# Softmax factors of an attention block sent through device memory instead of through matmuls, in a fused attention and two-layer MoE kernel

## The chip, the core and the metric

One core of one Trainium2 chip runs the kernel. The metric is the device time of one execution in microseconds. The kernel before took 609.13 us (median of three runs, 607.92 to 609.83).

## What is computed

Causal attention over 2 batches, 12 heads, 448 positions and 64 values a head; then two feed-forward blocks over the 896 tokens. All is float32 at the ends.

```python
def _attn_ref(q, k, v):
    scores = scale * np.matmul(q, k.transpose(0, 1, 3, 2))
    scores = np.where(mask, -1000000000.0, scores)
    scores = scores - np.max(scores, axis=-1, keepdims=True)
    attn = np.exp(scores)
    attn = attn / (np.sum(attn, axis=-1, keepdims=True) + 1e-09)
    return np.matmul(attn, v).astype(np.float32)
```

The first block is x @ w_in (768 to 2048), a clipped square, @ w_out; the second normalizes by the root of the mean square, multiplies silu(x @ w_gate) by x @ w_val (768 to 1536) and goes through w_out2.

The change is about one factor of this, 1 / (sum of the exponentials + 1e-9): one number for each head and query position.

## The kernel before

The attention goes by **groups** g of two heads (j = 0, 1), twelve in all. The 448 positions are cut into four chunks c of 112. A group is done in three **units** u = 0, 1, 2 (chunk 3; chunks 2 and 0; chunk 1), and a loop over n = 3g + u issues, in one iteration, steps of several units: the scores of unit n + 1 (TensorE, L267), the maxima of unit n (VectorE, L274) and its exponentials with their sums (ScalarE, L282), the copies out of PSUM of unit n − 2 (L316 on ScalarE, L318 on VectorE), and the transposes of unit n − 1 (TensorE, L298). With u = 2 the product with v of the group before is issued (`pv`, L346), which needs all its transposed exponentials. The order on each engine is the order of the code; nothing is reordered. Scores turn through four PSUM banks, two for each unit, so the scores of a unit need the exponentials of the unit two before to be done; the transposes and the spread turn through three other banks (`tring`).

The factor takes this way. With u = 0 VectorE adds 1e-9 to the sums and takes the reciprocal (`factor`, L324 and L325): a tile `rs` of 112 partitions (positions within a chunk) by 2 heads by 4 chunks. But the product with v stands with 64 partitions for each head and the positions along the row, so the factor is needed as a row, the same on 64 partitions. With u = 1 `spread` (L332) does this by eight matmuls: a column of `rs`, repeated 64 times, against the identity matrix. Each appears as two matmul instructions in the trace, 16 for a group. ScalarE copies the result to `rb` (L334). With the next u = 0 `xsplit` multiplies the product with v by `rb` on VectorE (L352), in place, and GpSimd splits it into a high and a low part (L353, L354), inputs of the first block.

SP issues all DMAs, in the order of the code, and holds at each one until what it waits for is there: q and k of a group two ahead (L239, L240, with u = 1, when the scores have read the buffer), v (L234, after `pv`), and weight blocks of 768 KB (L137), each when a stage buffer is free. While the attention runs, a few weight blocks are already loaded and split (L157 to L190), a share of a block in each group. From the last unit on, matmuls of the first block (L361) are issued between the attention's steps, and then the blocks follow: L361, L551, L666.

Of the kernel before, what the change touches and what calls it, by code (L numbers as in the profile page):

```python
# [10 lines left out]
F32 = mybir.dt.float32  # L11
# [4 lines left out]
ALU = mybir.AluOpType  # L16
# [24 lines left out]
def kernel(  # L41
# [14 lines left out]
    nc = tc.nc  # L56
    B, H, D, S = qT.shape
    P = 128
    C = 112
    NCH = S // C  # L60
# [14 lines left out]
    small = ctx.enter_context(tc.tile_pool(name="small", bufs=4))  # L75
    psum = ctx.enter_context(tc.tile_pool(name="psum", bufs=1, space=bass.MemoryType.PSUM))

    pst = psum.tile([P, 8, 512], F32, name="ps")

    def bank(n):  # L80
        return pst[:, n]

    ident = const.tile([P, P], F32, name="ident")
# [10 lines left out]
    TMO = STO + NST * 2 * NK * P  # L94
    AF = Arena(const, TMO + 2 * S, F32, "af")
# [6 lines left out]
    X = [AR.at(XO + h * 2 * NK * S, 2, NK, S) for h in range(2)]  # L102
    G = [AF.at(GO + h * NM * S, NM, S) for h in range(2)]
    stage = [AF.at(STO + i * 2 * NK * P, 2 * NK * P) for i in range(NST)]
    tmp = [AF.at(TMO + i * S, S) for i in range(2)]
# [11 lines left out]
    PTO = PO + 2 * NPC  # L117
    PTs = [AF.at(PTO + i * 2 * NTB * C, 2, NTB, C) for i in range(2)]
    XFO = PTO + 4 * NTB * C
    rb = AF.at(XFO, S)  # L120
    mask = AF.at(XFO + S, S)
    assert XFO + 2 * S <= STO
    poff = [0, C, 3 * C, 6 * C]
# [1 line left out]
    def b32(ap):  # L125
        return ap.bitcast(F32)
# [102 lines left out]
    NG = B * NP  # L229
    NN = NG * NU  # L230

    def load_v(g):
        if g < NG:
            nc.sync.dma_start(out=vraw[g % 2][:C], in_=v[g // NP, g % NP])  # L234
# [7 lines left out]
    def scale_q(g, eng):  # L242
        if g < NG:
            q = qraw[g % NQ]
            eng.tensor_scalar(out=q, in0=q, scalar1=float(D) ** -0.5, scalar2=1.0, op0=ALU.mult, op1=ALU.mult)  # L245

    sring = deque([0, 1, 2, 3])
    tring = deque([4, 5, 6])

    def turn(ring):  # L250
        ring.rotate(-1)
        return bank(ring[-1])
# [68 lines left out]
    def factor(g):  # L321
        sums = stat.pop(g)[1]
        rs = small.tile([P, 2, NCH], F32, tag="rs", name="rs")
        nc.vector.tensor_scalar(out=rs[:C], in0=sums[:C], scalar1=1e-9, scalar2=None, op0=ALU.add)  # L324
        nc.vector.reciprocal(rs[:C], rs[:C])  # L325
        return rs

    def spread(rs):
        t = turn(tring)
        for c in range(NCH):  # L330
            for j in range(2):
                nc.tensor.matmul(t[D * j:D * (j + 1), c * C:(c + 1) * C], lhsT=rs[:C, j, c:c + 1].to_broadcast([C, D]),  # L332
                                 rhs=ident[:C, :C], start=True, stop=True, skip_group_check=True)
        nc.scalar.copy(rb, t[:, :S])  # L334

    xbank = {}

    def pv(g):
        i = g % 2
        PT = PTs[i]  # L340
        xbank[g] = xb = bank(7)
        parts = [(0, 1, C, 3 * C), (0, 11, 0, C)] + [(kc, 4 * kc, kc * C, (NCH - kc) * C) for kc in range(1, NCH)]
        for n, (kc, blk, o, w) in enumerate(parts):
            for j in range(2):
                src = PT[:C, j].rearrange("p a d -> p (a d)")[:, blk * C:blk * C + w]
                nc.tensor.matmul(xb[D * j:D * (j + 1), o:o + w], lhsT=vraw[i][:C, j, kc, :], rhs=src,  # L346
                                 start=(n == 0), stop=(n == len(parts) - 1), skip_group_check=True)

    def xsplit(g):
        b, p = divmod(g, NP)  # L350
        xb = xbank.pop(g)
        nc.vector.tensor_tensor(out=rb, in0=xb[:, :S], in1=rb, op=ALU.mult)  # L352
        nc.gpsimd.tensor_scalar(out=X[b][:, 0, p], in0=rb, scalar1=1.0, scalar2=1.0, op0=ALU.mult, op1=ALU.mult)  # L353
        nc.gpsimd.tensor_tensor(out=X[b][:, 1, p], in0=rb, in1=b32(X[b][:, 0, p]), op=ALU.subtract)  # L354


    def mm3(out, w, x, ks=None):
# [88 lines left out]
    for n in range(last):  # L446
        g, u = divmod(n, NU)
        if n + 1 < NN:
            scores(n + 1)
        side = nc.vector if u == 2 else nc.scalar  # L450
        old = 2 <= n < NN + 2
        if u == 1:
            scale_q(g + 2, nc.gpsimd)
            load_qk(g + 3)
        if n < NN:
            maxima(n, 0)
            maxima(n, 1)
        if old and u == 1:
            evac(n - 2, 0, nc.scalar)
        if n < NN:  # L460
            exps(n, 0)
        if n < NN and u == 0:
            exps(n, 1)
        if old and u != 1:
            evac(n - 2, 0, nc.scalar)
            evac(n - 2, 1, side)
        if n < NN and u:
            exps(n, 1)
        if 0 < g < NG and u == 2:
            pv(g - 1)  # L470
            load_v(g + 1)
        if 1 <= n <= NN:
            transposes(n - 1)
        if u == 0:
            if g > 1:
                xsplit(g - 2)
            if g:
                frs = factor(g - 1)
        elif u == 1 and g:
            spread(frs)  # L480
            if g == NG:
                pv(g - 1)
        elif g == NG:
            xsplit(g - 1)
        if u == 2:
            w_pace(RATE[0])
        if n >= NN - 1:
            push_in(n - NN + 1, 0)
            pump(NK)
        flush()  # L490


    if True:
# [65 lines left out]
        rs = AF.at(4 * S, S)  # L559
# [98 lines left out]
        for dm in range(NK):  # L658
            w_need(2 * NM + 2 * NF + 2 * dm + 2)
            for h in range(2):  # L660
                w_pace(1)
                ob = nbank()
                for kk in range(NF):
                    x = (A0, A1)[h][kk]
                    for i, (a, c) in enumerate(((0, 0), (0, 1), (1, 0))):
                        nc.tensor.matmul(ob[:, :S], lhsT=w2[dm][:, kk // NK, a, kk % NK], rhs=x[:, c],  # L666
                                         start=(kk == 0 and i == 0), stop=(kk == NF - 1 and i == 2))
# [47 lines left out]
```

## Time and profile before

| | |
|---|---|
| median of the runs | 609.13 us (607.92 to 609.83) |
| span of the profiled execution | 607.3 us |
| matmuls busy | 597.2 us, 98% |
| VectorE busy | 385.7 us, 64% |
| ScalarE busy | 287.0 us, 47% |
| GpSimd busy | 162.9 us, 27% |
| share of the DMA engines | 32.5% on the queue of SP |

The span is the time from the first to the last instruction of one execution; the time of a run also holds what lies around it. [...] PE is the matmuls, PEld the weight loads, DVE VectorE, ACT ScalarE, POOL GpSimd, SP the engine that issues the DMAs. The attention takes about the first 110 us of the span, the rest is the two blocks. [...]

### The profile page before, as it was taken

The page shows a single profiled execution, that of the slowest core. Times are in us where ns is not written, and L with a number is a line of the kernel's source. Part 1 is how long each engine was busy: PE and PEld are TensorE (multiplying, and loading weights), DVE is VectorE, ACT ScalarE, POOL GpSimd, SP SyncE. Part 2 cuts the span into 40 slices and gives each one's busy share as a digit, 9 for nine tenths or more (in the row PEclk, how much of TensorE's full clock was granted, in tenths as well). Part 3 has the DMA queues.
Part 4 walks back from the last instruction along what each step waited for, and adds up shares of the span by engine and source line. Part 5 has one row for each costly group of instructions (what it writes and reads, how often), then busy time and mean ns, then how long its engine had stood idle before and what let it go on. Part 6 is the DMA issues. An engine that isn't in the chain of part 4 may idle for free.

```text
span 607.3 us, 8643 instructions
## 1 busy us (share of the span) xinstructions
PE 597.2 (98%) x3316; PEld 524.9 (86%) x3316; DVE 385.7 (64%) x643; ACT 287.0 (47%) x567; POOL 162.9 (27%) x118
## 2 busy tenths in 40 slices
PE   6999999999999999999999999999999999999997
PEld 4666668899999989998899999999999999999996
DVE  4777784368787646655694688887767666964000
ACT  4888886266766744445433433343333333543100
POOL 3234242324344313230122103222222222132200
PEclk9999999999999999999999999999999999999999
DMA  8245322034454523431132103334333333182100
GB/s 305 83 140 145 93 84 68 0 105 158 163 201 155 165 81 120 158 104 53 52 105 97 59 1 104 105 112 140 113 104 105 104 105 105 52 254 91 38 30 32
DMA packets 16698, 65.06 MB, mean 107 GB/s; under 512 B 2000, under 2 KB 6608, under 8 KB 16656
## 3 DMA queue, kind: packets, MB, share of 16 engines
q1 hardware_dynamic: 16656, 64.50, 32.5%
q8 instruction: 26, 0.43, 0.3%
q14 instruction: 16, 0.13, 0.1%
HBM read 61.74 MB, written 2.75 MB: 106 GB/s over the span
## 4 chain that ended last, share of the span: by engine, by line
PE 97%; DVE 1%; ACT 1%; DMA 0%; issue 0%; SPq 0%; DVEq 0%; ACTq 0%
PE ps L361 48%; PE ps L551 18%; PE ps L666 14%; PE ps L267 5%; PE ps L298 5%; PE ps L346 4%; PE ps L332 2%; DMA af<-in_qT 0%; PE ps L577 0%; DVE ar L568 0%; ACT af L369 0%; DVE ps L163 0%; DVE af L176 0%; DVE ps L157 0%; ACT ar L504 0%
## 5 line engine op out<-in xcount | busy, mean ns | idle before, releaser
L361 PE MATMUL ps<-ar 128*128 128x448 f32 x1440 | 293.3, 366 | 0.0
L361 PEld LDWEIGHTS ps<-ar 128*128 128x128 f32 x1440 | 270.3, 188 | 21.8 <-issue 0.4
L190 POOL TENSOR_TENSOR ar<-af,ar 128x768 fp32r<-128x768 f32 x68 | 128.7, 1892 | 346.6 <-ACT ar L182 346.6
L551 PE MATMUL ps<-ar 128*128 128x448 f32 x576 | 118.1, 366 | 0.4 <-DVE ar L568 0.3
L551 PEld LDWEIGHTS ps<-ar 128*128 128x128 f32 x576 | 108.0, 188 | 10.2 <-DVE ar L568 0.9
L182 ACT CAST ar<-af 128x768 fp32r<-128x768 f32 x68 | 60.2, 886 | 98.5 <-DVE af L176 95.6
L666 PE MATMUL ps<-ar 128*128 128x448 f32 x432 | 87.7, 365 | 0.0
L666 PEld LDWEIGHTS ps<-ar 128*128 128x128 f32 x432 | 81.2, 188 | 6.4
L172 ACT ACTIVATE af<-af 128x768 f32<-128x768 f32 x62 | 56.7, 914 | 25.5 <-DMA af<-in_w_out 15.2
L163 DVE SCALAR_TENSOR_TENSOR ps<-af,ps 128x768 int32<-128x768 int32 x62 | 59.6, 961 | 12.2 <-ACT af L172 9.6
L157 DVE TENSOR_SCALAR ps<-af 128x768 int32<-128x768 int32 x62 | 59.1, 953 | 8.2 <-DMA af<-in_w_out 6.5
L176 DVE SCALAR_TENSOR_TENSOR af<-af,ps 128x768 int32<-128x768 int32 x62 | 59.1, 954 | 5.3
L282 ACT ACTIVATE af<-ps,nm 112x336 f32<-112x336 f32 (+2 forms) x96 | 46.9, 502 | 8.5 <-DVE nm L274 8.5
L274 DVE CUSTOM_DVE_ANT_0 ps<-ps,af 112x336 f32<-112x336 f32 (+2 forms) x96 | 41.5, 473 | 12.2 <-PE ps L267 11.1
L505 DVE TENSOR_TENSOR ar<-af,ar 128x448 fp32r<-128x448 f32 x32 | 23.3, 732 | 40.3 <-ACT ar L504 40.3
L374 DVE SCALAR_TENSOR_TENSOR af<-af,ps 128x448 f32<-128x448 f32 x32 | 19.8, 618 | 38.8 <-ACT af L370 38.8
L504 ACT CAST ar<-af 128x448 fp32r<-128x448 f32 x32 | 18.0, 566 | 49.8 <-PE ps L551 49.8
L267 PE MATMUL ps<-af 64*112 64x448 f32 (+3 forms) x192 | 36.2, 462 | 4.6 <-DVE af L245 4.4
L369 ACT ACTIVATE af<-ps,half 128x448 f32<-128x448 f32 x32 | 20.1, 628 | 26.1 <-PE ps L361 26.1
L669 ACT COPY af<-ps 128x448 f32<-128x448 f32 x12 | 6.4, 533 | 53.5 <-PE ps L666 27.4
L298 PE MATMUL ps<-ident,af 112*112 112x112 f32 x240 | 31.6, 272 | 0.0
L298 PEld LDWEIGHTS ps<-ident,af 112*112 112x112 f32 x240 | 23.8, 137 | 8.0 <-issue 4.2
(52 smaller groups left out, 381.4 us busy)
## 6 DMA issues: line engine op xcount, KB each, us to landing
af<-in_w_out SPq DMA_DIRECT2D x28, 768.0 KB, 4.3
af<-in_w_in SPq DMA_DIRECT2D x16, 768.0 KB, 4.3
af<-in_w_gate SPq DMA_DIRECT2D x12, 768.0 KB, 4.2
af<-in_w_val SPq DMA_DIRECT2D x12, 768.0 KB, 4.2
af<-in_kT SPq DMA_DIRECT2D x12, 224.0 KB, 2.7
af<-in_qT SPq DMA_DIRECT2D x12, 224.0 KB, 3.1
af<-in_v SPq DMA_DIRECT2D x12, 224.0 KB, 2.6
out_T<-af SPq DMA_DIRECT2D x12, 224.0 KB, 2.0
```

Source lines behind the costliest of these rows:

```text
L157: nc.vector.tensor_scalar(out=out, in0=t, scalar1=29, scalar2=0, op0=ALU.logical_shift_right, op1=ALU.bitwise_or)
L163: nc.vector.scalar_tensor_tensor(out=t, in0=words(n, 1, I32), scalar=-2 ** 31, in1=t, op0=ALU.bitwise_and, op1=ALU.bitwise_or)
L172: nc.scalar.mul(c, c, 2.0 ** -112)
L176: nc.vector.scalar_tensor_tensor(out=words(n, 0, I32), in0=words(n, 1, I32), scalar=3, in1=part.pop(n), op0=ALU.logical_shift_left, op1=AL ...
L182: nc.scalar.copy(dst[:, 0, :], value(n))
L190: nc.gpsimd.tensor_tensor(out=dst[:, 1, :], in0=value(n), in1=b32(dst[:, 0, :]), op=ALU.subtract)
L267: nc.tensor.matmul(bs[j][:C, o:o + (c + 1) * C], lhsT=q[r, c * C:(c + 1) * C], rhs=k[r, :(c + 1) * C], start=True, stop=True, skip_group_c ...
L282: nc.scalar.activation(Pn[:C, j, poff[c]:poff[c] + w], sbank[n][j][:C, o:o + w], ACTF.Exp, bias=nm[:C, j, c:c + 1], scale=-1.0, accum_out= ...
L298: nc.tensor.transpose(bs[j][:C, o:o + C], Pn[:C, j, poff[c] + kc * C:poff[c] + (kc + 1) * C], ident[:C, :C])
L361: nc.tensor.matmul(out, lhsT=w[:, a, k * P:(k + 1) * P], rhs=x[:, c, k], start=(k == 0 and n == 0), stop=(k == NK - 1 and n == 2))
L551: nc.tensor.matmul(ybs[dm][:, :S], lhsT=w[:, a, dm * P:(dm + 1) * P], rhs=t[:, c], start=(n == 0 and i == 0), stop=(n == NM - 1 and i == 2))
L666: nc.tensor.matmul(ob[:, :S], lhsT=w2[dm][:, kk // NK, a, kk % NK], rhs=x[:, c], start=(kk == 0 and i == 0), stop=(kk == NF - 1 and i == 2))
```

## The change

`spread` with its matmuls and its copy is gone. `factor` itself sends `rs` to a buffer in device memory, `row`, two heads by 448 numbers, of which there are two in turn. The position of a number in a row is p·4 + c (p within a chunk, c the chunk), so each partition writes four numbers in one piece: 112 partitions by two heads give 224 pieces of 16 bytes. Two loads, one for each head, read a row back with a partition step of zero: 64 partitions get the same 448 numbers. The target is one of two buffers, `rbs`; one is the old `rb`, the other lies in a temporary row of the first block, `tmp[1]`. The loads wait for the store. `xsplit` reads the factor in steps of four numbers (the order of the rows) and writes its product to `tmp[0]`, not in place.

```diff
+    dram = ctx.enter_context(tc.tile_pool(name="dram", bufs=2, space=bass.MemoryType.DRAM))
...
-    rb = AF.at(XFO, S)
+    rbs = [AF.at(TMO + S, S), AF.at(XFO, S)]
...
         nc.vector.reciprocal(rs[:C], rs[:C])
-        return rs
-
-    def spread(rs):
-        t = turn(tring)
-        for c in range(NCH):
-            for j in range(2):
-                nc.tensor.matmul(t[D * j:D * (j + 1), c * C:(c + 1) * C], lhsT=rs[:C, j, c:c + 1].to_broadcast([C, D]),
-                                 rhs=ident[:C, :C], start=True, stop=True, skip_group_check=True)
-        nc.scalar.copy(rb, t[:, :S])
+        row = dram.tile([2, S], F32, tag="row", name="row")
+        nc.sync.dma_start(out=row.rearrange("j (p c) -> p j c", c=NCH), in_=rs[:C])
+        for j in range(2):
+            nc.sync.dma_start(out=rbs[g % 2][D * j:D * (j + 1)], in_=row[j].partition_broadcast(D))
...
-        nc.vector.tensor_tensor(out=rb, in0=xb[:, :S], in1=rb, op=ALU.mult)
-        nc.gpsimd.tensor_scalar(out=X[b][:, 0, p], in0=rb, scalar1=1.0, scalar2=1.0, op0=ALU.mult, op1=ALU.mult)
-        nc.gpsimd.tensor_tensor(out=X[b][:, 1, p], in0=rb, in1=b32(X[b][:, 0, p]), op=ALU.subtract)
+        rb = rbs[g % 2]
+        xn = tmp[0]
+        nc.vector.tensor_tensor(out=xn.rearrange("p (c i) -> p c i", c=NCH),
+                                in0=xb[:, :S].rearrange("p (c i) -> p c i", c=NCH),
+                                in1=rb.rearrange("p (i c) -> p c i", c=NCH), op=ALU.mult)
+        nc.gpsimd.tensor_scalar(out=X[b][:, 0, p], in0=xn, scalar1=1.0, scalar2=1.0, op0=ALU.mult, op1=ALU.mult)
+        nc.gpsimd.tensor_tensor(out=X[b][:, 1, p], in0=xn, in1=b32(X[b][:, 0, p]), op=ALU.subtract)
...
             if g:
-                frs = factor(g - 1)
-        elif u == 1 and g:
-            spread(frs)
-            if g == NG:
-                pv(g - 1)
+                factor(g - 1)
+        elif u == 1 and g == NG:
+            pv(g - 1)
```

The line numbers of the changed kernel are a few off: scores L269, transposes L300, `pv` L343, `xsplit` L351, the store L329, the loads L331.

On TensorE, around the end of unit 1 of a group, there stood before (transposes, spread, scores of the next group, product with v):

```order
L298 MATMUL ps<-ident,af 112x112 x8
L332 MATMUL ps<-ident,rs 64x112 x8
L267 MATMUL ps<-af 112x448 x2
L346 MATMUL ps<-af 64x336 x2
L346 MATMUL ps<-af 64x112 x2
```

and now:

```order
L300 MATMUL ps<-ident,af 112x112 x8
L269 MATMUL ps<-af 112x448 x2
L343 MATMUL ps<-af 64x336 x2
L343 MATMUL ps<-af 64x112 x2
```

The eight matmuls of the spread are gone from between transposes and scores; nothing else moved.

On SP, in a group in which a weight block is loaded (`in_w_in`), there stood before:

```order
L234 DMA af<-in_v 112x512
L137 DMA af<-in_w_in 128x1536
L239 DMA af<-in_kT 128x448
L240 DMA af<-in_qT 128x448
L234 DMA af<-in_v 112x512
```

and now, with the store to `row` and the two loads from it:

```order
L236 DMA af<-in_v 112x512
L139 DMA af<-in_w_in 128x1536
L329 DMA row<-rs 112x2x4
L331 DMA af<-row 64x448 x2
L241 DMA af<-in_kT 128x448
L242 DMA af<-in_qT 128x448
L236 DMA af<-in_v 112x512
```

The three new DMAs stand behind the weight block and ahead of the loads of k and q.

## Rows read from the trace of the kernel before

**Rows 1.** The chain that ended last, shares of the span by line.

```profile
PE ps L361 48%; PE ps L551 18%; PE ps L666 14%; PE ps L267 5%; PE ps L298 5%; PE ps L346 4%; PE ps L332 2%; DMA af<-in_qT 0%; PE ps L577 0%; DVE ar L568 0%; ACT af L369 0%; DVE ps L163 0%; DVE af L176 0%; DVE ps L157 0%; ACT ar L504 0%
```

**Rows 2.** Stretches: length, busy of PE, PEld, DVE, ACT, POOL; clock, DMA share, GB/s.

```profile
60.00:80.00 20.00, 20.00 (x184) 13.46 (x180) 15.41 (x54) 16.36 (x52) 8.41 (x10) 1.00 0.34 96
...
300.00:400.00 100.00, 100.00 (x493) 92.37 (x492) 76.94 (x96) 37.38 (x57) 19.06 (x11) 1.00 0.26 86
```

**Rows 3.** The chain in order of time, two groups' spreads: start, length, what.

```profile
56.52 0.92 PE ps L332 x16
...
64.37 0.92 PE ps L332 x16
```

**Rows 4.** Timeline of PE in moments around starts of scores: start, length of all, count.

```profile
57.37 0.73 PE L267 MATMUL ps<-af 64*112 64x448 f32 x2
...
61.36 0.53 PE L267 MATMUL ps<-af 64*112 64x336 f32 x1
...
61.36 0.54 PE L267 MATMUL ps<-af 64*112 64x336 f32 x2
...
65.22 0.63 PE L267 MATMUL ps<-af 64*112 64x448 f32 x1
...
65.22 0.73 PE L267 MATMUL ps<-af 64*112 64x448 f32 x2
```

**Rows 5.** Timeline of VectorE and ScalarE, maxima and exponentials of unit 1.

```profile
62.40 0.52 DVE L274 CUSTOM_DVE_ANT_0 ps<-ps,af 112x336 f32<-112x336 f32 x1 [0.83 <-PE ps L267]
...
64.05 0.14 DVE L274 DVE_READ_ACCUMULATOR2_ANT nm<- 112x1 f32 x1
...
65.06 0.21 ACT L282 ACTIVATION_READ_ACCUMULATOR af<-ps,nm 112x1 f32 x1
65.39 0.53 ACT L334 COPY af<-ps 128x448 f32<-128x448 f32 x1
```

**Rows 6.** The spread's line: count, ns of one, first and last start.

```profile
L332 PE MATMUL ps<-ident,rs x192: 259/259/310, 17.1 to 107.9; 112*64 112x112 f32 x192
```

**Rows 7.** Timeline of PE and ScalarE around the last two spreads.

```profile
95.72 0.99 PE L332 MATMUL ps<-ident,rs 112*64 112x112 f32 x16
96.53 2.06 PE L346 MATMUL ps<-af 112*64 112x336 f32 x20
...
109.02 2.11 PE L346 MATMUL ps<-af 112*64 112x336 f32 x20 [0.83 <-ACT af L316]
...
108.45 0.51 ACT L316 COPY af<-ps 112x448 f32<-112x448 f32 x1
```

**Rows 8.** Timeline of VectorE, product with the factor and the reciprocal behind it.

```profile
60.63 0.62 DVE L352 TENSOR_TENSOR af<-ps,af 128x448 f32<-128x448 f32 x1 [0.96 <-ACT af L282]
...
61.37 0.20 DVE L325 RECIPROCAL rs<-rs 112x8 f32<-112x8 f32 x1
```

**Rows 9.** Landings: gvec; out_T from 545 us; out_T 531 to 545; v 20 to 95.

```profile
gvec<-in_rms_g SPq DMA_DIRECT2D x1, 3.0 KB, 5.1
...
DMA to landing us min/median/max: 1.9/1.9/3.8
...
DMA to landing us min/median/max: 4.7/5.0/5.0
...
DMA to landing us min/median/max: 2.4/2.6/2.9
```

**Rows 10.** SP: DMA issues of a group with a weight block; the three blocks' landings.

```profile
54.27 0.33 SPq L137 DMA_DIRECT2D af<-in_w_in  x1
...
60.56 0.33 SPq L234 DMA_DIRECT2D af<-in_v  x1
...
L137 SPq DMA_DIRECT2D af<-in_w_in x3: 328/328/328, 30.7 to 77.8; - x3
...
DMA to landing us min/median/max: 4.0/4.3/4.5
```

**Rows 11.** The costliest groups: a line that reads SBUF in steps of two.

```profile
L157 DVE TENSOR_SCALAR ps<-af 128x768 int32<-128x768 int32 x62 | 59.1, 953 | 8.2 <-DMA af<-in_w_out 6.5
```

## The prediction

> **What bounds the kernel now.** I read the chain of waits first, by line [rows 1]: matmuls almost alone, and L332, the matmuls that spread 1/sum, has 2% of the span, about 12 us. Taken at its word, this is what the change removes. So the second view is the busy time by stretch [rows 2]: TensorE counts as busy for 20.00 of 20 us at 60 to 80 us (and in the three other stretches between 20 and 100), but its weight loads fill only 13.46 us of these, against 92.37 of 100 us later. TensorE is full in the later stage; in the attention something may stand in its queue without showing as a gap. [...] By matmul busy time alone rival A below would be the forecast.
>
> The third view settles it for me: single instructions of one group of two heads, of which there are twelve, 7.85 us apart in the steady part (56.52 and 64.37) [rows 3]. A scores product is issued as two halves, j=0 and j=1, on two halves of the array. Where nothing holds them they start together: at 61.36 two matmuls cover 0.54 us where one covers 0.53. At 65.22, behind the spread, they don't: one covers 0.63, two cover 0.73, so j=1 started 0.10 us after j=0, at 65.32 [rows 4]. What it waits for is in its program: its bank must have been read by the exponentials of the unit two before. ScalarE ends these at 65.06 + 0.21 = 65.27 [rows 5]. So at the end of the spread TensorE is not late; ScalarE is, by 0.1 us.
>
> This closes a loop without the spread in it. TensorE runs from the j=1 product before (57.37 + 0.10 = 57.47) through L346, transposes and the next scores without a pause until 62.40, 4.93 us; VectorE, idle for 0.83 us before, then takes the maxima until 64.05 + 0.14 = 64.19; ScalarE takes the exponentials, released by them, until 65.27; then the next j=1 starts at 65.32 [rows 4, 5]. 4.93 + 1.79 + 1.08 + 0.05 = 7.85 us: the whole period. The spread, 0.92 us from 56.52 and from 64.37 [rows 3], lies beside the last two terms.
>
> **The change, part by part.** *Sixteen matmul instructions fewer in each group* (192 in all, 0.92 us a group) [rows 3, 6]. In the steady groups TensorE comes to the scores 0.92 us earlier, j=0 starts earlier, j=1 at the same 65.32, and L346 behind both at the same time: gain 0. Two groups at the end have no scores behind the spread. At 95.72 it is followed by L346 at 96.53, which TensorE issues at once: gain 0.81 us, passed on, because the stages behind it run on TensorE (100.00 of 100 us) [rows 2, 7]. At 107.20 it is followed by L346 at 109.02, which waits 0.83 us for ScalarE's copy L316 of 108.45; that one stands behind work on the product before, so the last spread is covered: gain 0 [rows 7]. The 0.81 itself does move all of this earlier.
>
> *ScalarE's copy L334*, 0.53 us in each group, follows the exponentials at 65.39 [rows 5]; it is not in the loop. Gain 0, since ScalarE waits later for VectorE anyway.
>
> *The turn of the banks.* The transposes now share three banks at five turns a group instead of six. Each bank that is reused was emptied as early as before or earlier; no cost.
>
> *Three DMAs in each group.* SP issues a store of 3.5 KB (224 runs of 16 bytes) when the reciprocal ends, waits for its landing, issues two loads of 112 KB each, and only then the next kT and qT loads. VectorE's L352 of the next group waits for the loads. Reciprocals end at 61.37 + 0.20 = 61.57; L352 stands at 60.63 + 7.85 = 68.48 [rows 8]. The cover is 6.91 us. No such store is in the trace. Nearest is out_T, 224 KB to the same memory, 1.9 us (median of nine) with no load right ahead of it; the other end is gvec, runs of 24 bytes and 5.1 us, but loaded behind six other transfers [rows 9]. I take 2.0, since here only a v load stands ahead, at 60.56, which lands in 2.6. A load of half the size of v takes 2.6 at most with nothing ahead; 1.9 at least. So store and loads together: 0.05 + 2.0 + 0.05 + 0.38 (second issue) + 2.6 = 5.1 us, bounds 4.3 and 8.2 (store 5.1). At 5.1 nothing waits: cost 0. The kT and qT loads slip by some 1 us; their readers come almost a group later.
>
> *Three groups have a weight load ahead.* SP issues w_in at 30.7, 54.27 and 77.8, and in the new order the store stands behind it [rows 10]. They land after 4.0 to 4.5 us; with 4.5 that of 54.27 at 58.8. Of a smaller transfer behind such a load there is a row: out_T at 531 to 540 lands in 4.7 to 5.0 instead of 1.9 [rows 9, 10]. So the store, issued at 54.65, lands at about 59.0 (by the out_T row 59.6), the loads go out at 59.05 and 59.43 and land at about 61.7 to 62.0. L352 would stand at 60.63: about 1.1 to 1.4 us late, and 0.83 of this is VectorE's idle time before the maxima [rows 5, 8]. The loop has no slack, so the rest stays: 0.25 us (the lower of the two, since w_in lands sooner in the other two) for each of the three, 0.7 in all. Bounds: 0, if the loads land as fast as out_T; and 4, with the store by the out_T row at 59.6 (loads at 62.6, 1.2 us beyond the cover) and a slower L352 (below).
>
> *L352 reads 1/sum in steps of four values.* It takes 0.62 us now, with steps of one; L157 reads in steps of two and takes 0.95 us for 768 values, no more for each value [rows 8, 11]. Steps of four are not in the trace. Bounds: 0, and 0.47, one more pass of 448 values at the 1.04 ns a value that lie between L157 and L352 ((953 − 620) / (768 − 448)). I take 0, since the nearest row shows no price. In a steady group up to 0.83 is covered; in the three groups it adds, which is in the 4. [...]
>
> **Sum.** Profiled execution: span 607.3; the median of the runs, 609.13, lies 1.8 above it. 607.3 − 0.8 + 0.7 = 607.2, and with the 1.8 **609.0 us**.
>
> **Rivals.**
> A, TensorE is the bound in the attention: the busy digits and the chain speak for it [rows 1, 2], the 0.10 us of j=1 against it [rows 4]. Then nearly every spread pays: 12 × 0.92 = 11.0 us, 598.1. If ScalarE follows partly, something between.
>
> B, the round trip is longer than its cover, and this ends on the slower side. L352 then waits for the loads, the next reciprocal comes 61.57 − 60.63 = 0.94 us after it, and store and loads start again: a loop of its own, of round trip + 0.94. It decides from 6.91 us on. With the store at gvec's 5.1 the round trip is 8.2, the period 9.1 instead of 7.85; over ten groups (the last two have over 10 us) 13 us: about 622. For it: 16-byte runs are nowhere in the trace. Against it: the transfers without a load right ahead land in 1.9 and 2.6 us, store and load [rows 9]. [...]
>
> C, only the three groups with a weight load pay, but in full: 607.3 − 0.8 + 4 + 1.8 = 612.3.
>
> That the matmuls and copies are not really gone is excluded: the order of instructions has none, and nothing in their place on TensorE.
>
> **Chances.** Forecast 0.64, A or a part of it 0.12, B 0.12, C 0.12. The range of 8 in 10 takes in the forecast, C, and the near parts of A and B: 605.5 to 614. A measurement can tell about 0.3% (1.8 us) from no change: faster 0.13 (A, and a little of the forecast), same 0.63, slower 0.24 (B, C).
>
> **What would show it.** After: the period between two scores products still 7.85 us, and now an open gap of about 0.8 us on TensorE before the j=1 product, released by ScalarE's exponentials. Steady groups: L352 not waiting for a DMA. Three groups: L352 waiting about 1 us for the loads, and the period some 0.3 longer there. Store landing near 2 us, near 4.5 behind w_in. A is right if the period falls to about 7; B if L352 waits in every group and the period is round trip + 0.94. I am wrong at the root if j=1's 0.10 us comes from something other than ScalarE.

## The result, and the profile after

The changed kernel takes **616.82 us** (median, 614.07 to 619.75); the kernel before took 609.09 us beside it. The ratio is 1.0137, with a 95% interval of 1.0116 to 1.0158: 1.4% slower, 7.7 us. The forecast was 609.0 with a range up to 614.0; the time lies above the range. Executions of one and the same kernel, the one before included, come in two lengths about 6 us apart (in a profiled execution of the longer kind, in experiment 8, a matmul of the first block takes 0.368 us where it takes 0.366 before), so a range below that reaches 615 us for a kernel of 609 holds some of each.

The profiled execution took 617.72 us with a span of 615.8, 8.5 more than the 607.3 of before. The page of the changed kernel, the chain that ended last by engine and by line (in the changed kernel L269 is the scores, L343 the product with v, L351 the multiplication by 1/sum, L329 the store and L331 the two loads):

```profile
PE 89%; DMA 4%; DVE 3%; ACT 1%; POOL 1%; issue 1%; SPq 0%; DVEq 0%; ACTq 0%
PE ps L362 47%; PE ps L550 18%; PE ps L665 14%; PE ps L269 4%; PE ps L343 4%; DMA row<-rs 2%; PE ps L300 2%; DMA af<-row 2%; DVE af L351 1%; POOL ar L355 1%; DMA af<-in_qT 0%; DVE ps L276 0%; PE ps L576 0%; ACT af L284 0%; POOL ar L354 0%
```

Beside [rows 1] the spread's 2% are gone, and the two new transfers stand in the chain with 2% each. So the new transfers end last in places.

Where? The same stretches as in [rows 2], and the two around the first and the second loss cut finer (length, busy time of PE, PEld, DVE, ACT, POOL, granted clock, DMA share, GB/s):

```profile
40.00:60.00 20.00, 17.87 (x111) 10.26 (x111) 14.02 (x50) 13.19 (x43) 8.34 (x10) 0.83 0.42 114
60.00:80.00 20.00, 17.20 (x116) 10.04 (x115) 12.99 (x44) 11.92 (x43) 5.38 (x8) 0.91 0.41 121
...
32.00:42.00 10.00, 7.92 (x59) 4.60 (x56) 6.04 (x25) 6.17 (x23) 2.40 (x3) 1.00 0.47 139
42.00:48.70 6.70, 6.65 (x25) 3.12 (x26) 3.15 (x10) 3.55 (x13) 0.57 (x1) 0.50 0.31 103
48.70:60.00 11.30, 11.16 (x86) 7.13 (x87) 8.94 (x31) 8.62 (x26) 6.27 (x7) 1.00 0.51 124
60.50:72.70 12.20, 9.47 (x61) 5.15 (x62) 7.50 (x27) 7.69 (x28) 2.64 (x4) 1.00 0.39 119
72.70:76.00 3.30, 3.30 (x17) 1.84 (x18) 2.14 (x5) 1.64 (x6) 0.00 (x0) 0.50 0.59 162
```

Two things stand there that before had nowhere between 20 and 100 us; the kernel before, beside its line of 60 to 80 in [rows 2]:

```profile
20.00:40.00 20.00, 20.00 (x186) 13.28 (x181) 14.63 (x52) 16.21 (x51) 9.27 (x11) 1.00 0.39 121
40.00:60.00 20.00, 20.00 (x188) 13.14 (x189) 16.18 (x56) 17.59 (x60) 7.24 (x9) 1.00 0.45 132
80.00:100.00 20.00, 20.00 (x193) 13.84 (x193) 13.42 (x48) 16.32 (x55) 4.87 (x7) 1.00 0.15 51
```

TensorE stands: 7.92 us busy of the 10 before 42. And behind such a stretch its granted clock is 0.50 (half clock, below): for 6.83 us from 41.96, and for 3.41 from 72.68.

What does TensorE wait for? The multiplication L351 by VectorE, one in a steady group and the three late ones:

```profile
28.45 0.99 DVE L351 TENSOR_TENSOR af<-ps,af 128x448 f32<-128x448 f32 x1 [1.05 <-PE ps L343]
29.36 0.17 DVE L326 TENSOR_SCALAR rs<-sums 112x8 f32<-112x8 f32 x1
29.56 0.20 DVE L327 RECIPROCAL rs<-rs 112x8 f32<-112x8 f32 x1
30.23 0.52 DVE L276 CUSTOM_DVE_ANT_0 ps<-ps,af 112x336 f32<-112x336 f32 x1 [0.48 <-PE ps L269]
...
38.75 0.97 DVE L351 TENSOR_TENSOR af<-ps,af 128x448 f32<-128x448 f32 x1 [3.86 <-DMA af<-row]
...
67.68 0.95 DVE L351 TENSOR_TENSOR af<-ps,af 128x448 f32<-128x448 f32 x1 [4.56 <-DMA af<-row]
...
94.16 0.97 DVE L351 TENSOR_TENSOR af<-ps,af 128x448 f32<-128x448 f32 x1 [3.03 <-DMA af<-row]
```

In the steady group L351 waits for TensorE's product with v and for no transfer; in three groups it waits for the loads of 1/sum. At 38.75 it is 2.45 us later than one period behind the row of 28.45 (36.30). Behind it on VectorE stand the maxima of the second unit, behind these ScalarE's exponentials, behind these the next scores: j=1 in a steady group, both halves where the wait is long. TensorE, the same places:

```profile
39.09 0.98 PE L300 MATMUL ps<-ident,af 112*112 112x112 f32 x8
42.05 2.64 PE L269 MATMUL ps<-af 64*112 64x448 f32 x4 [1.98 <-POOL ar L355]
44.62 4.00 PE L343 MATMUL ps<-af 112*64 112x336 f32 x20
...
70.95 1.44 PE L269 MATMUL ps<-af 64*112 64x448 f32 x3 [2.66 <-POOL ar L355]
72.69 3.77 PE L343 MATMUL ps<-af 112*64 112x336 f32 x20
...
97.45 0.97 PE L269 MATMUL ps<-af 64*112 64x448 f32 x2 [1.15 <-POOL ar L355]
```

The releaser in brackets is not the one: POOL's L355 had long ended. ScalarE's exponentials of the second unit, which the scores need, end just ahead of the start: those of j=0 at 41.75 + 0.20 = 41.95, ahead of 42.05. Twenty matmuls L343 take 4.00 us at half clock; [rows 7] has them at 2.11.

The transfers of the first of these groups: the weight load (29.34), the store (29.79) and the two loads (35.20); and a store of a group without a weight load (21.9), each with its time from issue to landing:

```profile
L139 SPq DMA_DIRECT2D af<-in_w_in x1: 327/327/327, 29.3 to 29.3; - x1
...
DMA to landing us min/median/max: 5.7/5.7/5.7
...
L329 SPq DMA_DIRECT2D row<-rs x1: 349/349/349, 29.8 to 29.8; - x1
...
DMA to landing us min/median/max: 5.4/5.4/5.4
...
L331 SPq DMA_DIRECT2D af<-row x2: 450/519/588, 35.2 to 35.7; - x2
...
  DVE af L351: 3.9, 1
...
DMA to landing us min/median/max: 2.8/2.8/2.9
...
L329 SPq DMA_DIRECT2D row<-rs x1: 339/339/339, 21.9 to 21.9; - x1
...
DMA to landing us min/median/max: 2.5/2.5/2.5
```

With no weight load ahead, the store lands in 1.5 to 2.7 us (3.0 in the first group, behind the loads of the start). Behind a weight load it lands in 5.4, 4.8 and 4.8 us (29.79, 58.00, 86.01), 0.16 to 0.56 us after the weight load itself.

**Where the 8.5 us are.** As a clock for the attention I take the start of the second half, j=1, of the first unit's scores in each group, the point at which the prediction closed its loop. Read from the single instructions, in us (the MoE is the two feed-forward blocks; its first matmul is the first of L361, L362 in the changed kernel):

```
group        0     1     2     3     4     5     6     7     8     9    10    11   first MoE matmul
before    4.41 11.20 18.20 26.05 33.91 41.76 49.62 57.47 65.33 73.18 81.03 88.88   99.27
after     4.32 10.54 17.45 25.31 33.16 42.86 53.53 61.39 71.76 81.54 89.40 98.26  107.88
period, after (from group 3)  7.86  9.70 10.67  7.86 10.38  9.78  7.86  8.86
```

Start-up, to group 3: −0.74. Three groups whose multiplication waits for the loads (periods 9.70, 10.38, 8.86): 1.84 + 2.52 + 1.01 = **5.4 us**. Two groups that run on half clock behind them (10.67, 9.78): 2.81 + 1.92 = **4.7 us**; 0.26 of the second is not the clock's, since the same group takes 8.11 in experiment 1, at a granted clock of 1.00 and with no transfer of 1/sum. The end of the attention: 9.62 instead of 10.39, −0.77. The MoE: +0.1. Together +8.7 at the last matmul; 8.5 in the span. The rest of the groups have the old period. The −0.74 is not the change's: two executions of one and the same kernel among those below (the thirds) have their group 3 at 26.12 and at 24.67.

### The profile page after: what moved, and what is told of

The parts are those of the page before. It is cut to its first block, busy times and chain, and to the rows that moved or that the text cites. A ratio compares the mean times of both kernels' runs of the same rounds, so it can differ in the third digit from the quotient of the medians.

```text
span 615.8 us, 8312 instructions
## 1 busy us (share of the span) xinstructions
PE 597.8 (97%) x3124; PEld 518.2 (84%) x3124; DVE 387.9 (63%) x643; ACT 282.3 (46%) x555; POOL 164.2 (27%) x118
## 4 chain that ended last, share of the span: by engine, by line
PE 89%; DMA 4%; DVE 3%; ACT 1%; POOL 1%; issue 1%; SPq 0%; DVEq 0%; ACTq 0%
PE ps L362 47%; PE ps L550 18%; PE ps L665 14%; PE ps L269 4%; PE ps L343 4%; DMA row<-rs 2%; PE ps L300 2%; DMA af<-row 2%; DVE af L351 1%; POOL ar L355 1%; DMA af<-in_qT 0%; DVE ps L276 0%; PE ps L576 0%; ACT af L284 0%; POOL ar L354 0%
## 5 line engine op out<-in xcount | busy, mean ns | idle before, releaser
L362 PE MATMUL ps<-ar 128*128 128x448 f32 x1440 | 293.3, 366 | 0.0
L362 PEld LDWEIGHTS ps<-ar 128*128 128x128 f32 x1440 | 270.2, 188 | 21.8 <-issue 0.4
L269 PE MATMUL ps<-af 64*112 64x448 f32 (+3 forms) x192 | 44.1, 455 | 11.9 <-POOL ar L355 5.8
L269 PEld LDWEIGHTS ps<-af 64*112 64x112 f32 x192 | 18.7, 182 | 27.8 <-ACT af L284 7.3
L318 ACT COPY af<-ps 112x448 f32<-112x448 f32 x48 | 24.5, 539 | 18.6 <-PE ps L300 18.6
L343 PEld LDWEIGHTS ps<-af 112*64 112x64 f32 x240 | 16.6, 150 | 19.2 <-issue 3.3
```

Source lines behind the costliest of these rows:

```text
L269: nc.tensor.matmul(bs[j][:C, o:o + (c + 1) * C], lhsT=q[r, c * C:(c + 1) * C], rhs=k[r, :(c + 1) * C], start=True, stop=True, skip_group_c ...
L362: nc.tensor.matmul(out, lhsT=w[:, a, k * P:(k + 1) * P], rhs=x[:, c, k], start=(k == 0 and n == 0), stop=(k == NK - 1 and n == 2))
```

## Experiments

In each, "theory Q" is that the store, standing behind a weight load, makes the loads and so the multiplication late, and that the rest follows from this. Periods are those of j=1 as above.

**1. The spread away, nothing in its place.** The kernel before with a constant factor in place of 1/sum; the product goes to `tmp[0]`, as in the changed kernel.

```diff
     def spread(rs):
-        t = turn(tring)
-        ... 16 matmuls
-        nc.scalar.copy(rb, t[:, :S])
+        return
...
+    nc.gpsimd.memset(rb, 0.01)
```

> The kernel before with the spread's matmuls and ScalarE's copy taken out and nothing in their place: the factor is a constant row (so 1/sum isn't applied), no new DMA. Theory Q (the store waits in SP's queue behind a weight load, the loads come late, VectorE's product waits, and TensorE stands behind it): the matmuls lie beside the loop through VectorE and ScalarE, so the period of a group stays 7.85 us, only one spread near the end pays 0.8 us: 607.5 to 609, clock 1.00 in all stretches. Rival M (TensorE's new gap of 0.9 us in each group lets its clock fall): granted clock under 1 in the attention, 612 or more. Rival A of the prediction (TensorE bounds the attention): period near 7, 598.

Measured: 608.50 us (607.18 to 609.62, ten runs), ratio 0.9985 [0.9960, 1.0009]; span 606.9, clock 1.00 in every stretch, periods 7.85 but for one of 8.11, end of the attention 9.62.

```profile
40.00:60.00 20.00, 19.58 (x140) 11.32 (x141) 15.30 (x56) 16.82 (x58) 7.24 (x9) 1.00 0.40 133
60.00:80.00 20.00, 19.62 (x151) 12.12 (x148) 14.58 (x52) 14.61 (x47) 8.81 (x11) 1.00 0.33 98
```

So the 192 matmuls and 12 copies are worth nothing in the steady groups, and without them alone the clock doesn't fall. This is also the most that taking them away could bring with the rest as it is, and it can't be told from nothing here: rivals A and M fall, and the loss belongs to what was put in their place.

**2. Weight loads behind the loads of 1/sum.** The changed kernel, where in the attention a weight load that has become due is issued behind the next two loads of 1/sum.

```diff
-        w_load(n + NST)
+        if hold[0]:
+            late.append(n + NST)
+        else:
+            w_load(n + NST)
...
                 factor(g - 1)
+            while late:
+                w_load(late.pop(0))
...
+            hold[0] = n < NN - 1
             w_pace(RATE[0])
+            hold[0] = False
```

> The changed kernel, but the weight load that stood ahead of the store in three groups is issued behind the two loads of the factor. Theory Q: the product with the factor waits for no DMA, the period is 7.85 us in every group, clock 1.00, 607.5 to 609. Rival M: the clock still falls, 612 or more. Rival K (the three DMAs delay the loads of q and k, and TensorE waits for these): they still stand ahead of k and q in every group, so the long periods stay, 613 or more.

Measured: 611.64 us (608.50 to 614.99, ten runs), ratio 1.0037 [1.0006, 1.0068]; about 5 of the 7.7 us are gone. Profiled: 609.99, span 607.9; six steady periods of 7.85, then 8.87, 9.49 and 7.85. The two long ones have the same cause as before, one step further on: a weight load is issued at 56.6, kT and qT behind it, and the store at 60.8 behind all of them.

```profile
L139 SPq DMA_DIRECT2D af<-in_w_in x1: 523/523/523, 56.6 to 56.6; - x1
...
DMA to landing us min/median/max: 6.4/6.4/6.4
...
L334 SPq DMA_DIRECT2D row<-rs x1: 334/334/334, 60.8 to 60.8; - x1
...
DMA to landing us min/median/max: 4.2/4.2/4.2
```

The direction is Q's, but the time lies between the ranges of Q and M, and the clock falls here too, to half for 3.4 us from 73.75 on, behind a gap of 0.90 us on TensorE. The edit moved the collision; it did not remove it. Over the ten runs the time goes with the mean granted clock: 608.5 to 609.4 us at 0.999 or 1.000 (three runs), 610.0 and 611.4 at 0.997, 611.9 to 615.0 at 0.994.

**3. The multiplication in steps of four, alone.** The kernel before, with the copy writing the factor in the order in which the new store has it and the multiplication reading it in steps of four.

```diff
-        nc.scalar.copy(rb, t[:, :S])
+        nc.scalar.copy(rb.rearrange("p (i c) -> p c i", c=NCH), t[:, :S].rearrange("p (c i) -> p c i", c=NCH))
...
+                                in1=rb.rearrange("p (i c) -> p c i", c=NCH), op=ALU.mult)
```

> The kernel before, with the factor laid down and read in steps of four values, as in the changed kernel; the spread and its copy stay. All theories: the product takes 0.97 us instead of 0.62, which the 0.83 us of VectorE's idle time before the maxima cover: period 7.85, 608 to 610. If the 0.35 us paid, 12 of them would give 613.

Measured: 609.23 us (608.53 to 610.03, ten runs), ratio 1.0001 [0.9978, 1.0025]. The longer multiplication (0.95 to 1.00 us) is hidden in the steady groups, with periods of 7.85. In the three groups with a weight load the period is 8.04: 0.6 us in all, too little to be told from nothing in the time.

**4. The spread's matmuls kept as filler.** The changed kernel with the 16 matmuls of each group left in; nothing reads them.

```diff
+    def spread(rs):
+        ... 16 matmuls as before, no copy
...
+        elif u == 1 and g:
+            spread(frs)
```

> The changed kernel, but the spread's matmuls stay on TensorE, their result unused (no copy). Theory Q: the product still waits in the three groups with a weight load, 5.7 us in all; TensorE stands 0.9 us less each time. If the half clock comes from standing nearly 2 us, it stays away and the time is 613 to 615; if not, 617 to 619. Rival M: clock 1.00 and no long period, 608 to 610.

Measured: 616.62 us (613.43 to 621.76, four runs), ratio 1.0120 [1.0042, 1.0198]; profiled 618.64, span 616.6. The waits remain: 9.06, 10.53 and 10.05 us, 6.1 more than three periods. Of the forecast's two cases each came: in two of the runs, 613.43 and 614.61, the mean granted clock is 0.999, so it did not fall; the fourth, 621.76 at 0.997, lies outside both. In the profiled run, 618.64, it falls once instead of twice:

```profile
40.00:60.00 20.00, 19.57 (x176) 12.56 (x176) 16.29 (x58) 15.70 (x54) 9.31 (x11) 1.00 0.47 139
60.00:80.00 20.00, 18.17 (x162) 11.60 (x160) 13.31 (x46) 13.34 (x44) 5.03 (x7) 1.00 0.45 129
...
95.00:102.20 7.20, 7.20 (x31) 3.82 (x30) 4.45 (x10) 3.15 (x12) 0.17 (x1) 0.53 0.20 40
```

So with the matmuls the clock falls less often (mean granted clock 0.994 to 0.999 in the four runs, 0.991 to 0.994 in those of the changed kernel; here not behind the first two waits), but they remove none of the waiting, and one fall at the end of the attention costs 3.3 us (13.66 instead of 10.39 to the first MoE matmul).

**5. The store in another queue.** The changed kernel; ScalarE issues the store.

```diff
-        nc.sync.dma_start(out=row.rearrange("j (p c) -> p j c", c=NCH), in_=rs[:C])
+        nc.scalar.dma_start(out=row.rearrange("j (p c) -> p j c", c=NCH), in_=rs[:C])
```

> The changed kernel with one edit: the store of 1/sum is issued by ScalarE and so goes through ScalarE's DMA queue, where nothing else stands; the two loads and all other transfers stay in SyncE's queue. Theory Q (in SyncE's queue the store of three groups lands behind a weight load of 768 KB): those three stores should land in some 1.5 to 3 us instead of 4.8 to 5.4. The two loads still go into SyncE's queue, but now while the weight load is under way, and so they could inherit the wait: they would then land when the weight load does, some 5.5 to 6 us after its issue, which the multiplication at L351 can just bear. If so, most of the 5.7 us of waits and of the 4.4 us of half clock go: 608 to 611. Rival E (it is the 16 DMA engines that are busy with the weight load, whatever the queue): store and loads land as late as in the changed kernel: 615 to 619.

Measured: 616.32 us (611.00 to 622.32, twelve runs), ratio 1.0102 [1.0070, 1.0134] over the ten runs under 620. Rival E: the store, now alone in its queue but issued at 28.8 behind a weight load of 28.3, lands after 4.4 us, 0.16 us after the weight load.

```profile
L139 SPq DMA_DIRECT2D af<-in_w_in x1: 328/328/328, 28.3 to 28.3; - x1
...
DMA to landing us min/median/max: 4.7/4.7/4.7
...
L329 ACTq DMA_DIRECT2D row<-rs x1: 321/321/321, 28.8 to 28.8; - x1
...
DMA to landing us min/median/max: 4.4/4.4/4.4
```

The packets say how. Time from the store's issue to the first and the middle one of its 224 packets of 16 bytes, and how many of the weight load's 128 packets had started by the first ("same queue" is the changed kernel, "other queue" this one; the first group's store is left out):

```
store                        first     middle     weight packets started
no weight load ahead       0.81-0.85  0.92-0.96   -
behind the load, same queue   3.05-3.09  3.42-3.57   103 to 108 of 128
behind the load, other queue  2.07-2.77  3.17-3.29    53 to 100 of 128
```

So it is not the order within SyncE's queue, as I had thought: in both cases the weight load's packets are mostly served first. By the store's middle packet 115 to 126 of the 128 had started, in the same queue 118 to 123. In the other queue the first packet comes earlier (2.07 to 2.77 us instead of 3.05 to 3.09), the middle one hardly (3.17 to 3.29 instead of 3.42 to 3.57); how the DMA engines divide their time between the two queues is not shown.

**6. The weight loads in the other queue.** Experiment 2 with the held-back weight loads issued by ScalarE.

```diff
-                w_load(late.pop(0))
+                w_load(late.pop(0), nc.scalar)
```

> The changed kernel with the weight loads of the attention issued by ScalarE, behind the loads of 1/sum, so that SyncE's queue holds only the store, the two loads and those of q, k and v. In the run with the weights behind in SyncE's queue one group still lost 0.8 us and the next 1.9: there the store issued at 60.78 us stood behind q and k, which stood behind the weight load, landed after 4.22 us, and the clock fell. Theory Q: with the weights in another queue that store lands in 1.5 to 3 us too, every period is 7.85 and the clock doesn't fall: 607.5 to 609.5, at or a little under the kernel before. Rival E (the engines, not the queue): the store of that group stays late, 610 to 613.

Measured: 616.90 us (614.13 to 617.69, six runs), ratio 1.0115 [1.0072, 1.0158]. The edit did something else than I meant: ScalarE doesn't wait, as SyncE does, for the store ahead, so the weight load went out at 29.5, again right ahead of the store of 30.0. That makes it a second measurement of experiment 5, with the queues exchanged: the store lands after 5.0 us, the weight load after 5.3, and the periods are those of the changed kernel (9.31, 10.81, 9.97, 9.75, 8.64). Again the order of issue counts and not the queue. What was to be tested, weight loads out of the way of a store issued 4 us later, this run doesn't show.

**7. Late by hand.** Experiment 1, so without any round trip (1/sum is not applied), with five more multiplications on VectorE ahead of the one in the three groups that wait in the changed kernel.

```diff
+        if g in (2, 5, 8):
+            for _ in range(5):
+                nc.vector.tensor_tensor(out=tmp[1], in0=xb[:, :S], in1=rb, op=ALU.mult)
         nc.vector.tensor_tensor(out=xn, in0=xb[:, :S], in1=rb, op=ALU.mult)
```

> The kernel without the spread (constant factor, 1/sum not applied, no DMA round trip; it took 608.5 us) with five extra VectorE multiplications of 128 x 448 ahead of the one at xsplit in three groups, the same three in which the changed kernel waits. That makes the multiplication some 2.6 to 3.0 us late, with no transfer in it. Theory Q with the clock as its consequence: TensorE stands about 2 us in each of the three, and its clock falls to half after one or more of them; three times 2.1 to 2.5 us of waits and 2 to 7 us of half clock: 616 to 622. Rival C1 (the half clock has another cause than TensorE's standing): the waits alone, 614.5 to 616, at granted clock 1.00 throughout. Rival C2 (a late multiplication alone doesn't hold up TensorE, and the loss came with the transfers): 608.5 to 611.

Measured: 621.46 us (620.18 to 623.08, six runs), ratio 1.0189 [1.0144, 1.0234]; span 621.2 against 606.9 in experiment 1. One of the three places, and the clock around it:

```profile
37.38 3.26 DVE L350 TENSOR_TENSOR af<-ps,af 128x448 f32<-128x448 f32 x5 [1.36 <-PE ps L341]
40.55 0.61 DVE L351 TENSOR_TENSOR af<-ps,af 128x448 f32<-128x448 f32 x1
...
43.48 1.58 PE L267 MATMUL ps<-af 64*112 64x448 f32 x3 [2.29 <-POOL ar L353]
...
33.50:43.50 10.00, 7.71 (x57) 4.58 (x57) 8.40 (x28) 5.86 (x21) 2.21 (x4) 1.00 0.44 142
43.50:50.20 6.70, 6.70 (x27) 3.10 (x28) 3.34 (x10) 3.48 (x13) 0.06 (x1) 0.59 0.00 0
```

The periods 10.01, 11.07, 7.85, 10.01, 10.80, 7.85, 10.01 have the pattern of the changed kernel (9.70, 10.67, 7.86, 10.38, 9.78, 7.86, 8.86). The multiplication is 3.17 us late (40.55 instead of 37.38); a group loses 2.2, and the group behind it another 3 on half clock. Both parts of the loss come with a late multiplication alone; C1 and C2 fall. Behind a gap of 2.29 us the granted clock is 0.59 over the next 6.70 us, with no transfer of 1/sum to blame: in this run the fall comes with the waiting.

**8. Weight loads in thirds.** As experiment 2, but a third of the load (256 KB) behind the two loads of 1/sum in each of three groups.

```diff
+                sl = slice(part * PIECE, (part + 1) * PIECE)
+                nc.sync.dma_start(out=stage[n % NST].bitcast(I32)[:, sl], in_=src.bitcast(I32)[:, sl])
...
-            late.append(n + NST)
+            late.extend((n + NST, part) for part in range(3))
...
-            while late:
-                w_load(late.pop(0))
+            if late:
+                w_load(*late.pop(0))
```

> The changed kernel with each weight load of the attention cut into three of 256 KB, one behind the two loads of 1/sum in each of three groups. The two runs with another queue showed that the store lands just behind the weight load whichever queue either is in, if it is issued behind it; so what counts is how many bytes of weights are still to come when the store is issued. Theory D (the DMA engines serve the earlier bytes first): a third of the load lands well before the next store, each store takes 1.5 to 2.7 us, no multiplication waits, every period is 7.85 and the clock stays at 1.00: 607.5 to 609.5. Rival R (the round trip itself, three more transfers in each group, costs something in every group): 610 to 613 with periods over 7.85 in groups without a weight load.

Measured: periods 7.85 to 7.86 but for one of 8.12, first MoE matmul at 98.86. The time, 614.78 us (607.08 to 616.50, twelve runs), ratio 1.0044 [1.0004, 1.0085], doesn't settle it: the profiled execution spends 513.91 us behind its first MoE matmul where before spends 508.00, and nothing was changed there. So the same kernel was measured again.

> The kernel with the weight loads in thirds once more. In its first runs all periods of the attention were 7.85 to 8.12 and the first matmul of the MoE stood at 98.86 us (before: 99.27), while each matmul of the MoE took 0.368 us instead of 0.366, which lengthened the rest by 5.5 us; about half of the runs of the kernel before beside it were as long. Theory D: what is left of the change then is the 0.4 us at the end of the attention: 607 to 609.5 where the MoE's matmuls take 0.366 us, ratio 0.996 to 1.001. Rival R (the thirds slow the MoE): 614 to 616 again, beside runs of the kernel before at 609.

Measured: **608.63 us** (607.59 to 615.02, twelve runs) beside 609.02, ratio 1.0002 [0.9983, 1.0021]; span 605.8. The nine thirds and the twelve stores:

```profile
L141 SPq DMA_DIRECT2D af<-in_w_in x9: 518/578/585, 31.8 to 95.3; - x9
...
DMA to landing us min/median/max: 3.0/3.3/4.0
...
L338 SPq DMA_DIRECT2D row<-rs x12: 324/338/347, 13.4 to 105.1; - x12
...
DMA to landing us min/median/max: 1.5/2.1/2.9
```

No store is over 2.9 us, the clock is 1.00 in every stretch, and periods are 7.85 to 7.86 but for 8.24 and 8.12. Behind the 8.24 stands one multiplication that still waits (at 60.24, for a load of 1/sum that takes 4.3 us with a third issued 0.7 us behind it). The whole loss is gone with all three transfers, their 16-byte packets and the steps of four still there: theory D, and rival R falls.

**9. The multiplication later.** The changed kernel, transfers untouched; the multiplication stands behind the second unit's maxima.

```diff
-            if g > 1:
+            if g == NG:
                 xsplit(g - 2)
...
+        if u == 1 and 1 < g < NG:
+            xsplit(g - 2)
```

> The changed kernel with the transfers untouched and the multiplication (xsplit) moved behind the maxima and the copy of the second unit, some 2.5 us later in VectorE's order; its store still lands behind the weight load in three groups. In the changed kernel the multiplication stood 1.6 to 3.2 us idle in those groups, and the second unit's maxima behind it. Theory D: what hurts is only that VectorE waits ahead of those maxima; behind them the multiplication has 2.5 us more, two of the three waits vanish and the third is under 1 us, and TensorE doesn't stand: 607.5 to 611. Rival P (the place behind the second unit's maxima is as tight, since the third unit's maxima stand behind it there): periods over 7.85 in all groups, each 0.3 to 1 us: 611 to 618.

Measured: 609.59 us (607.90 to 616.24, twelve runs) beside 609.29, ratio 1.0006 [0.9958, 1.0054]; span 607.2. Its stores still land late; the multiplication doesn't wait any more, and no period but one (8.59, in the group that takes 8.11 in experiment 1) is over 7.86:

```profile
63.45 0.95 DVE L351 TENSOR_TENSOR af<-ps,af 128x448 f32<-128x448 f32 x1
...
L329 SPq DMA_DIRECT2D row<-rs x12: 329/373/1326, 14.1 to 106.7; - x12
...
DMA to landing us min/median/max: 1.5/3.2/4.7
```

So a store of 4.7 us in itself cost nothing here. What cost was the place at which VectorE waited for it: ahead of the maxima that the loop runs through. Rival P falls.

**10. Both, thirds and later.** Experiments 8 and 9 together.

> Both remedies: weight loads in thirds behind the loads of 1/sum, and the multiplication moved behind the second unit's maxima. Theory D: each alone brought all or all but one of the periods back to 7.85, so nothing is left for the second to gain: 607 to 609.5, like the thirds alone and like the kernel before. Rival S (rests of waits under 0.3 us in each group, which neither remedy removes alone, still cost something): 605 to 607, faster than the kernel before.

Measured: 609.09 us (608.08 to 615.62, twelve runs) beside 609.02, ratio 1.0026 [1.0000, 1.0051]; one period of 8.58 again, the end of the attention 10.43 instead of 9.62, as in experiment 9. Nothing is left for the second remedy to gain; rival S falls. No version beats the kernel before.

## Why the prediction was wrong, by its own steps

*The loop of 7.85 us* was right, and more exactly than the sum needed. After, VectorE starts the maxima at 30.23 (row above), 25.31 + 4.92; j=1 starts at 33.16, 2.93 later. The prediction had 4.93 and 2.92. Four periods of the changed kernel (2 to 4, 6 to 7 and 9 to 10 in the table) and nearly all in experiments 1, 8 and 9 are 7.85 or 7.86 without the spread.

*Sixteen matmuls fewer: gain 0 in the steady groups* was right. The open gap of 0.8 us expected on TensorE is not to be seen as one, because j=0 runs in it by itself: of the four matmuls from 32.35 on, j=0's two start at 32.35 and 32.79, j=1's at 33.16.

```profile
32.35 1.82 PE L269 MATMUL ps<-af 64*112 64x448 f32 x4
34.09 0.79 PE L343 MATMUL ps<-af 112*64 112x336 f32 x4
```

*0.81 us at 95.72, 0 at the last spread* were right: −0.77 at the end of the attention, and the wait ahead of the last L343 has grown by the spread's length, 1.75 us instead of the 0.83 of [rows 7].

```profile
117.58 2.11 PE L343 MATMUL ps<-af 112*64 112x336 f32 x20 [1.75 <-ACT af L318]
```

*L334's copy, the bank ring, kT and qT behind the loads: 0* were right; experiment 8 has them all and loses nothing.

*Three DMAs in each group: cost 0* was right where no weight load is near, though the round trip is longer than the 5.1 us taken: store 1.5 to 2.7, loads 2.7 to 3.5, and 0.5 between the two loads' issues instead of 0.38; from the store's issue to the second landing 4.8 to 6.4 us in the seven groups between 20 and 108 us without a weight load ahead. The cover of 6.91 was enough there, by 0.5 us at the least. Rival B's condition was not met.

*Three groups have a weight load ahead* is the step that failed: 0.7 us in the sum, 5.4 measured as waits alone. The place and the mechanism of the wait were as foretold, the sizes not. The multiplication was forecast 1.1 to 1.4 us late; it was 2.45 late in the first group, 3.15 in the second (67.68, and 64.53 for one period behind 56.68) and 1.6 in the third (94.16, and 92.55 behind 84.69). The forecast had taken each term near its short end: weight loads landed in 4.7 to 5.7 us where I had 4.0 to 4.5 [rows 10]; from the first load's issue to the second's landing it took 3.4, 4.65 and 3.3 us where I had 2.7 to 3.0. The slower weight loads are not the work of the new transfers: experiment 1 has none, and there they land in 5.6, 4.6 and 5.2 us. In both kernels each is issued 0.9 us behind a load of v, before 1.6 us; that this is the reason is not shown. And the cover was counted whole, though part of it was gone. Of VectorE's 0.83 us idle [rows 5] 0.48 was left (row of 30.23), because of the next step.

*Steps of four: 0* was wrong; L351 takes 0.97 us against 0.62 [rows 8], +0.35. The nearest row (steps of two, no price) was the wrong neighbour, and 0.35 is inside the bound of 0.47 above. In a steady group it is hidden, in the three it is not (experiment 3). Why steps of four take longer is not shown.

*The clock* is the other failure, a term that the sum put at nothing without a reason. I read the granted clock of 1.00 in [rows 2] as a property of the stage; it was that of a TensorE that, once started, never stood longer than 0.83 us [rows 7]. In the changed kernel it was 0.50 for 6.83 us behind a gap of 1.98 us and for 3.41 us behind one of 2.66: another 4.7 us (4.5 without the 0.26 above), nearly as much as the waits. Rival C, the three groups paid in full, had 612.3 for the same wait; with the waits as measured (5.4 instead of 4) and the groups on half clock (4.7) it is 607.3 − 0.8 + 5.4 + 4.7 + 1.8 = 618.4, less 0.74 of start-up 617.7, the time of the profiled execution.

The bound on the slower side should have come from this: a loop without slack, a wait that can enter it, and a price for standing that is not the waiting alone. In the trace of before no row had that price; that is a reason for a range wide on the slower side, and mine reached only 1.7 us beyond C.

## What to carry to other kernels

A small transfer on whose landing an engine waits can take as long as the large one that was issued just ahead of it; here it did in either queue (the store 5.4 us behind a load of 5.7 in the same queue, 4.4 behind one of 4.7 in another). So look for what each large load is issued next to, and cut it up or move the reader behind the work that the loop needs, before counting a cover. Count a stall of TensorE twice in a range: once as the wait, and once as the half clock that may follow it, which cost nearly as much here (4.7 us beside 5.4). And work that hides beside a loop can be worth nothing when it is taken away, as the 12 us of matmuls here (608.50 us without them, ratio 0.9985): the first experiment, removing it with nothing in its place, tells how much there is to win.

## What the hardware showed that was not expected

- A 3.5 KB store of 16-byte runs lands in 1.5 to 2.7 us with no weight load ahead (changed kernel, behind the first group), and in 4.0 to 5.7 us when a 768 KB load was issued 0.4 to 0.6 us earlier, whether in the same queue (5.4, 4.8, 4.8; experiment 9: 4.0, 4.3, 4.7) or in another (4.4, 4.4, 5.7; exchanged 5.0, 4.9, 4.4). With 256 KB issued 4.1 to 5.4 us earlier, and landed by then, it takes 2.6 at most (experiment 8, second time, 31 to 98 us).
- TensorE's granted clock fell to 0.50 behind gaps of 1.98 and 2.66 us, but also behind one of 0.90 (experiment 2, 71.97), and not behind one of 0.98 (experiment 5, 40.04), of 1.15 (changed kernel, 97.45) or of 1.75 (changed kernel, 117.58; experiment 1, 108.52). The length of the gap alone does not tell; what does was not settled. In the kernels that wait the mean granted clock differs from run to run, and the time goes with it: in experiment 5 611.0 us at a mean granted clock of 0.997, 613.9 to 616.6 at 0.994, 617.1 to 618.5 at 0.989 to 0.992 (the ten runs of the ratio).
- VectorE multiplies 128x448 fp32 values in 0.97 us instead of 0.62 when one operand is read in steps of four (experiment 3, with the old transfers: 0.95 to 1.00).
- In the kernel before, the two halves of a scores product overlap (starts 0.10 us apart); where j=1 has to wait longer, j=0 runs through alone, and TensorE counts as busy in what is in truth a wait (changed kernel: j=0 from 32.35, j=1 at 33.16).
